# A new order of all operations of a gated recurrence with a highway layer behind it

## The chip, the cores and the metric

The kernel runs on one core of one Trainium2 chip. The metric is the device time of one execution in microseconds. The kernel before took 205.67 us, the median of 3 runs (205.38 to 205.77).

## The reference

The input is x (4 sequences of 6336 steps, 256 channels), gate logits of the same shape, and a lower bound per channel. The first half is a gated recurrence along each sequence; its result goes, token by token, through a highway layer with two 256x256 weights.

```
sig = sigmoid(f_logit)
f = lower_bound + (1 - lower_bound) * sig ; i = 1 - f
h = f[:, t] * h + i[:, t] * x[:, t] ; y[:, t] = h          # for t in 6336 steps, h = 0 at the start of each sequence
H = relu(y @ w_h) ; T = sigmoid(y @ w_t + b_t)
out = T * H + (1 - T) * y
```

## The kernel before

The 25344 tokens are cut into 29 units of 2, 4 or 8 blocks of 128 tokens (`parts`, L42): two units of 2 blocks, three of 4, twenty-two of 8, then one of 4 and one of 2. The 256 channels are two halves of 128; h or m (0 or 1) is the half. Every unit passes through the same operations, each of which is one short function, `do_` and a letter:

- l and x load the unit's logits and inputs (both queued on SP). One load fetches units 0 and 1 together.
- u (ACT): u = sigmoid(-logit), which is 1 - sig. b (POOL, or DVE): the product bv = u * x. Both have tokens on the partitions.
- i and p (PE): transposes of u and of bv, so that channels lie on the partitions (uT and bT, in PSUM).
- f (ACT, or DVE): f = 1 + ncc * uT, with ncc = lower_bound - 1 per channel.
- s (DVE): the recurrence, as a scan y = f * y + bT along the tokens. The factor 1 - lower_bound is left out of bv and comes in later, in the weights and in diag. A scan carries on from the scan of the same half in the unit before.
- z and g (PE): the two matmuls of the highway layer. Both need the y of both halves.
- t (ACT): t = sigmoid(z + b_t). d (DVE): d = max(ncc * y, g), which is relu(y @ w_h) - y, since the identity has been taken from w_h (IW, on POOL). e (POOL, or DVE): d = d * t, in pieces of 256 to 2048 columns.
- o (PE): transposes y and d back and adds them, through diag (cc on the diagonal) and an identity. c (ACT, or DVE): copies the result out of PSUM. w: the store, queued on SP (the very last one on ACT).

Besides there are single ones: the weight loads wh and wt, their scaling WH (DVE) and WTa (ACT), lbT and tbT (pc and pb: the bounds and biases turned), cc, cb, IW, dgp, and k, idle matmuls on PE.

What sets the order is a text of 847 tokens, `order`, written out by hand or by a search and read from left to right (L49 and L401). In `s4.1:2`, s is the operation, 4 the unit, 1 the half (or the piece), and 2 the buffer that its output takes. A `v` at the end puts b, f, e or c on DVE instead of POOL or ACT. `k*3:a0` is three idle matmuls into buffer a0. Each engine runs its operations strictly in the order of their tokens and waits only for data and for buffers. In PSUM, i and p share the two buffers a0 and a1, so a uT can be written when the scan has read the bT that lay there; z, g and o share b0, b1 and b2 (and in the last units a0 and a1). Six buffers hold l and six hold x. Loads and stores leave SP in the order of their tokens, and a store that waits for its c holds up the loads behind it.

One more rule is in `shared` (L173): after a product on DVE (b or e) the next product on POOL in the text waits until it is done.

Of the kernel before, what the change touches and what calls it, by code (L numbers as in the profile page):

```python
# [53 lines left out]
t2.0:2 b3.1:7 d2.0:2 e1.0 e0.0 x6:5 e2.0v p3.1:1 i4.0:0 s3.1:7 e0.1 l7:0 g2.1:0 u5:1 f4.0:0 z2.1:1 o1.0:2 i4.1:1 x7:0 t2.1 d2.1 i5.1:0
l8:1 b4.1:1 b4.0v:0 e2.1v g3.0:0 f4.1:2 x8:1 g3.1:1 i5.0:1 f5.1:1 p4.1:0 d3.0:1 d3.1 z3.0:0 s4.1:2 o0.0:1 l9:2 f5.0:3 c1.0:0 p4.0:1
z3.1:2 s4.0:3 t3.0:1 c0.0:1 t3.1 b5.1:2 u6:2 p5.1:0 b5.0:3 l11:3 x9:2 e3.0 z4.1:0 z4.0:1 t4.1:0 e3.1 t4.0 p5.0:1 s5.1:0 o2.0:2 s5.0:1
i6.1:0 g4.1:0 c2.0:2 f6.1:2 o3.0:1 d4.1:0 w0.0 w2.0 g4.0:2 b6.1:4 i6.0:1 c3.0:3 p6.1:0 w3.0 b6.0:5 u7:3 d4.0 f6.0:0 z5.0:0 g5.0:2
s6.1:4 d5.0:2 t5.0:2 z5.1:1 p6.0:0 i7.1:1 e4.0 b7.1:6 s6.0:5 f7.1:1 t5.1 g5.1:2 d5.1 p7.1:1 g6.1:0 i7.0:0 e4.1 o4.0:1 b7.0:7 u8:0
f7.0:3 c4.0:4 z6.1:2 e5.0 p7.0:0 s7.1:6 e5.1 b8.0:1 i8.1:1 d6.1:1 s7.0:7 t6.1:1 z6.0:1 e6.2 g6.0:0 d6.0 w1.0 f8.1:2 l10:4 i8.0:1
f8.0v:0 z7.0:2 u9:1 i9.1:0 t6.0 f9.1:1 g7.1:0 p8.0:1 x10:3 i9.0:0 l12:5 z7.1:1 e6.1v u11:2 f9.0:3 e5.2v e6.0v d7.1:0 t7.1:0 b8.1:0  # L60
s8.0:2 o6.1:0 c6.1:1 p8.1:0 o6.0:1 t7.0 i11.1:1 g7.0:0 b9.0:2 c6.0:2 u10:3 s8.1:3 d7.0 p9.0:0 f11.1:0 b9.1:3 e7.2 o5.0:2 c5.0:3 o5.1:1
g8.0:0 e7.1 p9.1:1 c5.1:0 s9.0:4 i10.0:0 x11:4 l14:0 l13:1 d8.0:1 z8.1:2 z8.0:1 f10.0:2 g8.1:0 t8.1:2 s9.1:5 b10.0:4 d8.1 p10.0:0
s10.0:0 w6.1 t8.0 b10.1:5 b11.1:6 e7.0 g9.1:2 i10.1:1 w4.0 z9.0:1 e8.1 u12:0 d9.1:2 w5.1 g9.0:0 f10.1:3 i11.0:0 t9.0:1 p10.1:1 x12:5
f11.0:1 l15:2 o7.1:1 w5.0 x13:0 b11.0:7 e8.2 u13:1 e8.0 d9.0 s10.1:1 z9.1:2 p11.1:0 o7.0:0 i13.1:1 t9.1 g10.0:2 c7.0:1 z10.0:0 s11.1:6
f13.1:2 i12.1:1 c7.1:4 b12.0:1 p11.0:0 t10.0:0 z10.1:1 d10.0:0 f12.1:3 g10.1:2 s11.0:7 d10.1 b12.1:0 t10.1 i12.0:1 e9.0v o8.1:0 g11.0:1
# [373 lines left out]
```

## Time and profile before

The profile is of one execution on the chip. Its own time was 205.4 us, 0.3 us under the median of the three runs; the span from its first to its last instruction is 203.6 us.

| | busy, us | instructions |
|---|---|---|
| PE (matmul) | 187.2 | 1784 |
| DVE | 191.4 | 154 |
| ACT | 193.6 | 202 |
| POOL | 172.7 | 104 |
| HBM | 52.43 MB read, 25.95 MB written | 385 GB/s over the span |

A row of the timeline gives start and length in us, engine, line, what is written from what, and in brackets the engine's idle time before it with what ended it. Lengths overlap: an instruction's record is some 0.05 to 0.4 us longer than the step to the next one's start when nothing waits, so steps from start to start are the better price. Rows of windows give busy time of PE, PEld, DVE, ACT and POOL with the count of instructions, the granted clock, the share of the DMA engines and GB/s.

### The profile page before, as it was taken

How to read it: one execution, taken by the hardware profiler on the slowest of the kernel's cores; microseconds unless marked ns; L12 is line 12 of the kernel's file. 1: busy time of each engine (PE TensorE's matmuls, PEld its weight loads, DVE VectorE, ACT ScalarE, POOL GpSimd, SP SyncE). 2: the span in 40 equal slices, each digit the busy share in tenths (PEclk: the TensorE clock that was granted, in tenths of full speed). 3: DMA queues.
4: the chain of work that ended last, by engine and by line, in shares of the span. 5: the costliest groups of instructions: out<-in, count | busy, mean ns of one | idle time of the engine just before them, and what ended most of it. 6: DMA issues, size and time to landing. Idle time of an engine off the chain costs nothing.

```text
span 203.6 us, 4577 instructions
## 1 busy us (share of the span) xinstructions
PE 187.2 (92%) x1784; PEld 130.9 (64%) x1812; DVE 191.4 (94%) x154; ACT 193.6 (95%) x202; POOL 172.7 (85%) x104
## 2 busy tenths in 40 slices
...
DMA  6999999999999999999999999999999996858876
GB/s 195 396 417 427 412 415 430 409 410 430 412 414 428 394 424 414 434 417 423 427 406 428 424 412 424 427 419 421 421 422 408 313 422 253 279 192 335 354 306 263
DMA packets 16381, 78.68 MB, mean 386 GB/s; under 512 B 1764, under 2 KB 2536, under 8 KB 10728
## 3 DMA queue, kind: packets, MB, share of 16 engines
...
q8 instruction: 14, 0.23, 0.4%
...
q14 instruction: 7, 0.06, 0.1%
HBM read 52.43 MB, written 25.95 MB: 385 GB/s over the span
## 4 chain that ended last, share of the span: by engine, by line
PE 44%; DVE 28%; ACT 10%; issue 8%; DMA 7%; SPq 0%; DVEq 0%; ACTq 0%
DVE y L323 17%; DVE d L352 7%; PE op L380 7%; PE op L381 6%; PE z L335 6%; PE g L335 6%; PE bT L304 6%; PE uT L284 5%; DMA out_dram<-o 5%; PE g L111 5%; PE z L111 4%; ACT f L295 3%; ACT u L268 3%; ACT t L348 2%; DMA x<-in_x_dram 2%
## 5 line engine op out<-in xcount | busy, mean ns | idle before, releaser
L276 POOL TENSOR_TENSOR bv<-u,x 128x1024 bf16<-128x1024 f16 (+2 forms) x54 | 103.9, 1945 | 12.6 <-DVE d L358 12.1
L323 DVE TENSOR_TENSOR_SCAN y<-f,y,bT 128x1024 bf16<-128x1024 f16 (+5 forms) x56 | 107.0, 1928 | 0.5 <-PE bT L304 0.4
L358 POOL TENSOR_TENSOR d<-d,t 128x512 bf16<-128x512 bf16 (+3 forms) x35 | 66.3, 1905 | 4.7 <-DVE d L358 3.5
L352 DVE SCALAR_TENSOR_TENSOR d<-y,ncc,g 128x1024 bf16<-128x1024 bf16 (+2 forms) x58 | 63.4, 1108 | 0.6 <-PE g L111 0.4
L348 ACT ACTIVATE t<-z,bt 128x1024 bf16<-128x1024 f32 (+2 forms) x58 | 62.3, 1105 | 0.5 <-PE z L111 0.2
L295 ACT ACTIVATE f<-uT,ncc 128x1024 f16<-128x1024 f16 (+2 forms) x55 | 60.6, 1112 | 0.9 <-PE uT L284 0.9
L393 ACT COPY o<-op 128x1024 f32<-128x1024 f32 (+2 forms) x56 | 53.5, 1010 | 1.4 <-PE op L381 1.4
L268 ACT ACTIVATE u<-l 128x2048 f16<-128x2048 f32 (+2 forms) x29 | 51.5, 1779 | 1.7 <-DMA l<-in_f_logit_dram 1.7
L380 PE MATMUL op<-diag,y 128*128 128x128 f16 x396 | 49.5, 219 | 1.2 <-DVE d L352 0.8
L381 PE MATMUL op<-ident_b,d 128*128 128x128 bf16 x396 | 49.6, 219 | 0.1
L381 PEld LDWEIGHTS <-d 128*128 128x128 bf16 x396 | 44.1, 113 | 4.4 <-issue 2.5
L380 PEld LDWEIGHTS <-y 128*128 128x128 bf16 x396 | 44.2, 113 | 2.0
L335 PE MATMUL z<-y,w_sb 128*128 128x512 bf16 (+1 forms) x112 | 38.9, 368 | 2.7 <-ACT t L348 0.7
L335 PE MATMUL g<-y,w_sb 128*128 128x512 bf16 (+1 forms) x112 | 38.7, 367 | 1.1 <-ACT o L393 0.7
L304 PE MATMUL bT<-ident_f,bv 128*128 128x128 f32 x198 | 31.9, 277 | 3.8 <-DVE y L323 1.4
L284 PEld LDWEIGHTS <-u 128*128 128x128 f16 x396 | 26.6, 98 | 11.2 <-issue 4.3
L284 PE MATMUL uT<-ident_h,u 128*128 128x128 f16 x396 | 31.4, 219 | 1.9 <-DVE y L323 1.7
L335 PEld LDWEIGHTS <-w_sb 128*128 128x128 f16 x232 | 22.0, 98 | 16.3 <-DVE y L323 0.9
L111 PE MATMUL g<-y,w_sb 128*128 128x512 bf16 x84 | 31.8, 379 | 0.1
L304 PEld LDWEIGHTS bT<-ident_f,bv 128*128 128x128 f32 x198 | 22.4, 141 | 12.8 <-issue 4.1
L111 PEld LDWEIGHTS <-w_sb 128*128 128x128 f16 x176 | 17.2, 98 | 17.4 <-issue 3.6
L111 PE MATMUL z<-y,w_sb 128*128 128x512 bf16 x72 | 27.3, 379 | 0.1
...
## 6 DMA issues: line engine op xcount, KB each, us to landing
out_dram<-o SPq DMA_DIRECT2D x48, 512.0 KB, 10.0
...
out_dram<-o SPq DMA_DIRECT2D x2, 256.0 KB, 16.0
...
```

The lines of the kernel that those rows point to most:

```text
L111: return pe.add_instruction(mybir.InstMatmult(name=nc.get_next_instruction_name(), start_tensor_calc=start, stop_tensor_calc=stop, tile_si ...
L276: shared(pin(e.tensor_mul(bv[:, :nb // 2].rearrange("p k d j -> p k j d"), st[n]["u"][:, :nb, own].rearrange("p (k j) d -> p k j d", j=2), ...
L284: pin(nc.tensor.transpose(uT[:, j * P:(j + 1) * P], st[n]["u"][:, j, h * P:(h + 1) * P], ident_h))
L295: pin(nc.scalar.activation(to, of, AF.Identity, scale=ncc[:, h:h + 1], bias=1.0))
L304: pin(nc.tensor.transpose(words[:, k:k + g * (P - 1) + 1:g], pair, ident_f))
L323: pin(nc.vector.tensor_tensor_scan(y[:, c:e], st[n]["f", h][:, c:e], st[n]["bT", h][:, c:e], 0.0 if fresh else carry[h], op0=ALU.mult, op1 ...
L335: pin(nc.tensor.matmul(p[:, a:e], w, half(n, "y", ki)[:, a:e], start=ki == 0, stop=ki == NH - 1))
L348: pin(nc.scalar.activation(half(n, "t", m), st[n]["z", m][:, :tokens(n)], AF.Sigmoid, bias=bt[:, m:m + 1]))
L352: pin(nc.vector.scalar_tensor_tensor(half(n, "d", m), half(n, "y", m), ncc[:, m:m + 1], st[n]["g", m][:, :tokens(n)], op0=ALU.mult, op1=AL ...
L358: shared(pin(e.tensor_mul(st[n]["d"][:, a:c], st[n]["d"][:, a:c], st[n]["t"][:, a:c])), not eng)
L380: pin(nc.tensor.matmul(o, half(n, "y", h)[:, cols], diag[:, h], start=True, stop=False))
L381: pin(nc.tensor.matmul(o, half(n, "d", h)[:, cols], ident_b, start=False, stop=True))
```

## The change

Only the text `order` is replaced, and it is one line longer, so all lines of the kernel behind it move by one. Both texts have the same 847 operations but for the idle matmuls. Units, buffers, rules and functions stay as they were. In the text

- all operations may stand at another place, and many take another buffer;
- on DVE instead of POOL are now b1.1, e5.1, e24.1 and e25.2, and on POOL instead of DVE e6.1, e26.2 and e27.0; f3.1 is on DVE instead of f2.1; c27.0 is on DVE instead of ACT;
- there are 15 idle matmuls instead of 12. Before: 3, 2, 2, 2, 2 among the first units and 1 at unit 14. After: 3 and 4 ahead of the first transpose, 2 and 2 among the first units, 3 and 1 at units 6 to 8;
- wt is loaded ahead of wh;
- the first stores stand behind l10 instead of ahead of it, and later loads and stores are interleaved in another order.

The first two lines of the text show what the diff is like:

```
-l0:0 k*3:a0 pc:0 cc k*2:a1 pb:1 k*2:a0 u0:0 x0:0 u1:1 b0.0v:0 wh i0.1:1 f0.1:0 i1.0:0 k*2:2 b0.1v:1 cb i0.0:1 f1.0:1 b1.0v:2 f0.0:2 wt
-IW p0.1:0 b1.1:3 WTa k*2:0 p0.0:1 s0.1:0 i1.1:0 l2:1 s0.0:1 p1.0:1 f1.1:3 WH x2:1 s1.0:2 u2:2 p1.1:0 g0.0:2 z0.1:1 i2.1:1 dgp l3:2
...
+l0:0 k*3:a0 u0:0 k*4:a1 x0:0 pc:0 cc i0.1:0 u1:1 i1.0:1 pb:1 wt f0.1:0 b0.1v:0 f1.0:1 k*2:2 i0.0:0 f0.0:2 WTa b1.0v:1 wh b0.0v:2
+b1.1v:3 cb l2:1 p0.1:1 IW k*2:0 p0.0:0 x2:1 s0.1:0 l3:2 i1.1:1 s0.0:1 f1.1:3 WH p1.1:0 x3:2 z0.0:2 g0.0:1 s1.1:2 u2:2 t0.0:0 p1.0:1
```

and the lines around unit 18, where the second bT (p18.1) follows the first z of unit 17 instead of both z and the uT i19.1:

```
-o14.0:0 s17.1:5 c14.1:4 p18.0:0 b19.0:6 i18.1:1 z16.1:1 d16.0 c14.0:0 f18.1:0 g17.1:2 t16.1 i20.0:1 z17.0:0 f20.0:3 w12.1 t17.0:2
-b19.1:7 s18.0:0 w13.0 b20.0:0 d17.1:1 z17.1:1 l22:3 e16.0v t17.1 i19.1:0 p18.1:1 w14.1 u21:0 x21:2 b20.1:1 w14.0 g17.0:2 o16.1:0
...
+w12.1 w11.0 x20:1 d15.1 u20:1 f19.0:0 o14.0:1 s17.1:5 c14.0:4 g16.0:0 p18.0:0 c14.1:2 i18.1:1 f18.1:2 d16.0 z16.1:1 g17.1:0 b20.1:0
+i20.0:1 t16.1 z17.0:2 s18.0:0 l21:2 d17.1:2 e16.0v w13.0 w12.0 w13.1 p18.1:0 s18.1:1 f20.0:3 i19.1:1 z17.1:1 t17.0:2 x21:2 f19.1:1
```

Three places of the built programs show how the engines' own orders move. First DVE in the head, from its first product on; bv is b, y is s, w_sb is WH, f is f, d is d. Before:

```order
L276 TENSOR_TENSOR bv_118<-u_112,x_114 128x2x128
L276 TENSOR_TENSOR bv_132<-u_112,x_114 128x2x128
L202 COPY bt_90<-tbT_107 128x2
L276 TENSOR_TENSOR bv_140<-u_116,x_114 128x2x128
L323 SCALAR_TENSOR_TENSOR y_158<-f_124,bT_147 128x256
L323 SCALAR_TENSOR_TENSOR y_165<-f_142,bT_156 128x256
L225 TENSOR_SCALAR w_sb_92<-w_raw_91,cc_88 128x256 x2
L323 SCALAR_TENSOR_TENSOR y_175<-f_138,y_165,bT_167 128x256
L323 SCALAR_TENSOR_TENSOR y_196<-f_169,y_158,bT_179 128x256
L293 TENSOR_SCALAR f_207<-uT_187,ncc_89 128x512
L352 SCALAR_TENSOR_TENSOR d_230<-y_165,ncc_89,g_181 128x256
L352 SCALAR_TENSOR_TENSOR d_232<-y_196,ncc_89,g_222 128x256
```

and with the change:

```order
L277 TENSOR_TENSOR bv_126<-u_100,x_107 128x2x128
L277 TENSOR_TENSOR bv_140<-u_116,x_107 128x2x128
L277 TENSOR_TENSOR bv_143<-u_100,x_107 128x2x128
L277 TENSOR_TENSOR bv_145<-u_116,x_107 128x2x128
L203 COPY bt_90<-tbT_121 128x2
L324 SCALAR_TENSOR_TENSOR y_161<-f_124,bT_150 128x256
L324 SCALAR_TENSOR_TENSOR y_168<-f_136,bT_157 128x256
L226 TENSOR_SCALAR w_sb_92<-w_raw_91,cc_88 128x256 x2
L324 SCALAR_TENSOR_TENSOR y_184<-f_170,y_161,bT_174 128x256
L324 SCALAR_TENSOR_TENSOR y_195<-f_128,y_168,bT_190 128x256
L353 SCALAR_TENSOR_TENSOR d_209<-y_168,ncc_89,g_181 128x256
L353 SCALAR_TENSOR_TENSOR d_209<-y_161,ncc_89,g_192 128x256
```

DVE makes all four products of units 0 and 1, and both d of unit 0 stand where an f of unit 2 and one d stood.

Second, DVE in the last units, from the d of unit 27 on (d_2998 and d_3028 are unit 27; d_3093 and d_3089 unit 28; a product d<-d,t is e). Before:

```order
L352 SCALAR_TENSOR_TENSOR d_2998<-y_2880,ncc_89,g_2979 128x512
L323 SCALAR_TENSOR_TENSOR y_3000<-f_2719,y_2880,bT_2996 128x256
L323 SCALAR_TENSOR_TENSOR y_3036<-f_2709,y_2939,bT_3023 128x256
L352 SCALAR_TENSOR_TENSOR d_2998<-y_2939,ncc_89,g_3038 128x512
L358 TENSOR_TENSOR d_2998<-d_2998,t_2977 128x512 x2
L352 SCALAR_TENSOR_TENSOR d_3093<-y_3036,ncc_89,g_3071 128x256
L352 SCALAR_TENSOR_TENSOR d_3093<-y_3000,ncc_89,g_3074 128x256
L358 TENSOR_TENSOR d_3093<-d_3093,t_3060 128x256 x2
```

and with the change:

```order
L353 SCALAR_TENSOR_TENSOR d_3028<-y_2923,ncc_89,g_3010 128x512
L353 SCALAR_TENSOR_TENSOR d_3028<-y_2990,ncc_89,g_3016 128x512
L324 SCALAR_TENSOR_TENSOR y_3068<-f_2687,y_2990,bT_3040 128x256
L359 TENSOR_TENSOR d_3028<-d_3028,t_3013 128x512
L353 SCALAR_TENSOR_TENSOR d_3089<-y_3068,ncc_89,g_3075 128x256
L392 COPY o_3107<-op_3078 128x512
L353 SCALAR_TENSOR_TENSOR d_3089<-y_2996,ncc_89,g_3101 128x256
L359 TENSOR_TENSOR d_3089<-d_3089,t_3087 128x256 x2
```

The last scan stands behind both d of unit 27, one e of unit 27 has gone, and the copy c27.0 stands between the two d of unit 28.

Third, the last operations of ACT (o<-op is c, t is t). Before:

```order
L348 ACTIVATE t_3060<-z_3057,bt_90 128x256
L393 COPY o_3054<-op_3062 128x512
L348 ACTIVATE t_3060<-z_3077,bt_90 128x256
L393 COPY o_3114<-op_3084 128x512
L393 COPY o_3114<-op_3095 128x512
L393 COPY o_3122<-op_3108 128x256
L393 COPY o_3124<-op_3116 128x256
```

and with the change:

```order
L349 ACTIVATE t_3087<-z_3071,bt_90 128x256
L394 COPY o_3107<-op_3092 128x512
L349 ACTIVATE t_3087<-z_3104,bt_90 128x256
L394 COPY o_3121<-op_3116 128x256
L394 COPY o_3129<-op_3123 128x256
```

c27.0 is no longer there, and c27.1 stands ahead of the last t, so that behind the last t only the two copies of unit 28 are left.

More of the change, by code (lines that the diff above doesn't have):

```diff
@@ L54 @@
[L54 to L65, printed above, removed]
@@ L90 @@
-p27.0:0 d25.1 s27.0:2 k*0:1 z26.0:1 c24.1:4 g26.1:0 e24.1 t26.0:2 b27.1:7 e25.0v d26.1:1 e25.2 o24.0:2 f27.1:2 p27.1:0 w23.0 w21.0
-b28.0:1 b28.1:2 c24.0:3 z26.1:1 s27.1:3 o25.2:a1 g26.0:0 e25.1v t26.1 o25.3:a0 d26.0 z27.1:2 w24.1 c25.2:2 z27.0:1 c25.3 t27.1:0
-g27.0:a1 e26.2v w23.1 t27.0 w24.0 e26.0v o25.1:0 p28.0:0 d27.0:0 s28.0:6 c25.1:1 e26.1 o25.0:2 o26.3:1 p28.1:1 c25.0 o26.2:0 w25.1
-s28.1:7 g27.1:2 c26.3:4 c26.2 d27.1 o26.0:1 c26.0:0 e27.0v z28.1:a0 t28.1:1 o26.1:a1 g28.1:0 g28.0:2 z28.0:1 w25.0 e27.1v c26.1 t28.0
@@ L94 @@
-o27.0:a0 d28.1:2 o27.1:0 d28.0 e28.1v e28.0v w26.1 o28.1:2 w26.0 c27.0:3 o28.0:a1 c27.1 c28.1:2 c28.0:1 w27.0 w28.1 w28.0
+l0:0 k*3:a0 u0:0 k*4:a1 x0:0 pc:0 cc i0.1:0 u1:1 i1.0:1 pb:1 wt f0.1:0 b0.1v:0 f1.0:1 k*2:2 i0.0:0 f0.0:2 WTa b1.0v:1 wh b0.0v:2
+b1.1v:3 cb l2:1 p0.1:1 IW k*2:0 p0.0:0 x2:1 s0.1:0 l3:2 i1.1:1 s0.0:1 f1.1:3 WH p1.1:0 x3:2 z0.0:2 g0.0:1 s1.1:2 u2:2 t0.0:0 p1.0:1
+g0.1:0 s1.0:3 l4:3 b2.1:4 i2.1:0 g1.0:2 d0.0:0 f2.1:0 d0.1 i2.0:1 d1.0:1 p2.1:0 l5:4 z1.1:1 s2.1:4 b2.0:5 f2.0:2 e0.0 z1.0:0 p2.0:1
```

65 lines of the change are left out of this document (41 added, 24 removed).

## The prediction

> **What bounds the kernel now.** I read the page first, then busy time by stage, then the first 30 us and the last 40 us of the timeline, then who waited for whom. Each fence shows one of these.
>
> ```profile
> PE 187.2 (92%) x1784; PEld 130.9 (64%) x1812; DVE 191.4 (94%) x154; ACT 193.6 (95%) x202; POOL 172.7 (85%) x104
> DMA  6999999999999999999999999999999996858876
> ```
>
> Three engines and the DMA queues are all above 90%, so the share says little. The stages tell more (columns: busy time of PE, PEld, DVE, ACT, POOL, clock, DMA share, GB/s):
>
> ```profile
> 24.00:159.00 135.00, 127.92 (x1233) 90.46 (x1254) 134.59 (x90) 135.00 (x124) 124.27 (x58) 1.00 1.02 419
> 159.00:199.00 40.00, 39.63 (x421) 29.74 (x425) 38.94 (x36) 38.14 (x48) 31.69 (x21) 1.00 0.81 306
> ```
>
> From 24 to 159 us ACT is busy 135.00 of 135.00: it paces this stage, with DVE 0.41 us behind. From 159 to 199 us the pacemaker is PE, 39.63 of 40.00, while ACT and DVE have 1.9 and 1.1 us free. So the span is a head, an ACT stage, a PE stage and a last store. What sets the head:
>
> ```profile
> 6.01 0.78 DVE L276 TENSOR_TENSOR bv<-u,x 128x256 bf16<-128x256 f16 x2 [1.65 <-DMA x<-in_x_dram]
> 10.08 2.29 POOL L276 TENSOR_TENSOR bv<-u,x 128x512 bf16<-128x512 f16 x2 [0.20 <-DMA x<-in_x_dram]
> 11.80 2.46 DVE L323 TENSOR_TENSOR_SCAN y<-f,y,bT 128x512 bf16<-128x512 f16 x2
> 8.69 0.33 SPq L256 DMA_DIRECT2D l<-in_f_logit_dram  x1
> DMA to landing us min/median/max: 15.2/15.2/15.2
> 23.99 1.94 ACT L268 ACTIVATE u<-l 128x2048 f16<-128x2048 f32 x1
> ```
>
> DVE starts at 6.01 because x0 lands. The first scan of unit 2 (11.80) follows the landing of x2, through POOL's product from 10.08. The load l6, issued at 8.69, takes 15.2 us and lands at 23.9; u6 starts at 23.99. From there ACT never rests.
>
> **The change part by part.**
>
> *Head.* The loads up to l11 keep their order and sizes; only the two 256 KB weight loads change places. All of them leave through one queue on DMA engines that are full from 5 us on, so x0, x2 and l6 should land as before: price 0. Between 6.01 and 11.80 DVE gets one more 256-wide product (b1.1, from POOL) and a third 256-wide d, and loses a 512-wide f (f2.1, now on ACT; f3.1 comes to DVE in its place, later):
>
> ```profile
> 7.28 1.26 DVE L323 TENSOR_TENSOR_SCAN y<-f,bT 128x256 bf16<-128x256 f16 x2
> 10.38 0.72 DVE L293 TENSOR_SCALAR f<-uT,ncc 128x512 f16<-128x512 f16 x1
> 11.02 0.86 DVE L352 SCALAR_TENSOR_TENSOR d<-y,ncc,g 128x256 bf16<-128x256 bf16 x2
> 21.66 6.93 DVE L323 TENSOR_TENSOR_SCAN y<-f,y,bT 128x512 bf16<-128x512 f16 x4 [0.18 <-PE bT L304]
> 29.88 2.35 DVE L323 TENSOR_TENSOR_SCAN y<-f,y,bT 128x1024 bf16<-128x1024 f16 x1
> 27.84 1.18 ACT L295 ACTIVATE f<-uT,ncc 128x1024 f16<-128x1024 f16 x1
> ```
>
> By start-to-start steps: +0.37 for b1.1, -0.64 for f2.1, +0.39 for the third d, so +0.1 before 11.80, where DVE had 0.1 to 0.2 of waits to give. Behind 11.80 it has 0.64 - 0.39 = 0.25 us more work and, in the old order, 0.4 us of waits up to 21.66. It meets the same wall at 29.88 in any case: s6.1 needs f6.1 (made from 27.84 on), which stands fourth behind u6 on ACT in both orders, and the bT whose buffer f6.1 frees. Head: 0, bounds -0.1 and +0.3.
>
> *Seven idle matmuls ahead of the lbT transpose instead of three* (and 15 in all instead of 12):
>
> ```profile
> 2.41 0.63 PE L122 MATMUL idle<-const-bfloat16-1.0 128*128 128x512 bf16 x1
> 2.84 1.06 PE L111 MATMUL idle<-const-bfloat16-1.0 128*128 128x512 bf16 x2
> 4.02 0.61 PE L122 MATMUL idle<-const-bfloat16-1.0 128*128 128x512 bf16 x1
> 5.17 0.39 PE L122 MATMUL idle<-const-bfloat16-1.0 128*128 128x512 bf16 x1
> 5.62 0.49 PE L284 MATMUL uT<-ident_h,u 128*128 128x128 f16 x4
> 5.93 1.31 ACT L295 ACTIVATE f<-uT,ncc 128x256 f16<-128x256 f16 x3 [0.23 <-PE uT L284]
> ```
>
> They stand 0.43 us apart until the clock is granted shortly before 5.17, and 0.22 after. Seven from 2.41 end at about 5.2; lbT and ncc follow by 5.6, before the first f (5.93) reads ncc. Cover: the wait for x0 until 6.01. If the clock came one matmul later the price is 0.2 us, and the landing of x2 hides that. Four more dummies at 38 to 41 us cost 0.9 us of a PE that has 7.1 us free in that stage. Price 0.
>
> *ACT stage.* Between u6 and the f that frees PE's bank for i24.1, ACT runs the same 123 operations in both orders, only permuted. With no idle time in it, a permutation gains nothing; it can lose where a uT, z or op comes late. DVE's one real wait in this stage goes away, since p18.1 now stands ahead of z17.1 and i19.1 on PE (1.3 us of work), but that gives DVE slack, not time:
>
> ```profile
> 124.85 2.35 DVE L323 TENSOR_TENSOR_SCAN y<-f,y,bT 128x1024 bf16<-128x1024 f16 x1 [0.25 <-PE bT L304]
> ```
>
> Price 0; bounds 0 and +0.3 (one DVE wait like this one turned into ACT's).
>
> *PE stage.* It begins when ACT has made f23.0:
>
> ```profile
> 157.60 1.35 ACT L295 ACTIVATE f<-uT,ncc 128x1024 f16<-128x1024 f16 x1
> 159.04 0.61 PE L284 MATMUL uT<-ident_h,u 128*128 128x128 f16 x8
> ```
>
> From i24.1 on both orders hold the same PE groups: 9 i, 11 p, 13 z, 14 g, 22 o. The old order leaves PE idle 0.37 us of 40.00 here, so a new one can gain 0.4 at most. I take 0; bounds -0.4 and +0.6, the latter from DVE, next.
>
> *DVE's last 19 us.* c27.0, a 512-wide copy out of PSUM, moves from ACT to DVE; e26.2 and e27.0 go to POOL, e24.1 and e25.2 come (four times 512, even).
>
> ```profile
> L391 DVE COPY o<-op 128x1024 f32<-128x1024 f32 x1 | 1.2, 1217 | 0.0
> 179.38 2.34 DVE L323 TENSOR_TENSOR_SCAN y<-f,y,bT 128x1024 bf16<-128x1024 f16 x1
> 183.13 2.34 DVE L323 TENSOR_TENSOR_SCAN y<-f,y,bT 128x1024 bf16<-128x1024 f16 x1
> 185.38 1.26 DVE L352 SCALAR_TENSOR_TENSOR d<-y,ncc,g 128x1024 bf16<-128x1024 bf16 x1
> 186.58 1.28 DVE L323 TENSOR_TENSOR_SCAN y<-f,y,bT 128x512 bf16<-128x512 f16 x1
> 191.53 1.28 DVE L352 SCALAR_TENSOR_TENSOR d<-y,ncc,g 128x1024 bf16<-128x1024 bf16 x1 [0.24 <-PE g L111]
> 197.96 0.49 DVE L358 TENSOR_TENSOR d<-d,t 128x256 bf16<-128x256 bf16 x2
> ```
>
> Half of the 1024-wide copy is about 0.62 us. From 179.38 to 198.45 DVE takes 19.07 us; its instructions by their unhindered steps (2.25 a 1024-wide scan, 183.13 to 185.38; 1.2 a 1024-wide d, to 186.58; and so on) come to 18.16, so 0.91 is waiting, mostly for PE. With the copy it has 18.78 of work: it fits in 19.07 if it waits no more than 0.29. I take that as hidden, price 0. If the old waits stay, +0.62.
>
> *The very end.*
>
> ```profile
> 198.16 0.30 DVE d L358
> 198.51 0.23 PE op L381
> 198.89 0.21 ACT o L393
> 199.11 0.54 ACT o L393 x2
> 198.03 1.63 ACT L393 COPY o<-op 128x512 f32<-128x512 f32 x4
> ```
>
> The last e ends at 198.45, PE's last op follows, but ACT is still in c27.1 until 199.0. Without c27.0, c27.1 is over before the last op is there (first op ready 198.8): -0.2 us. The store behind it stays.
>
> Sum against the profiled run: span 203.6 - 0.2 = 203.4, with the 1.8 us around it (205.4 - 203.6) 205.2. That run lies 0.27 under the median of 205.67, so the median forecast is 205.5.
>
> *A rule weighed.* In the trace the 512-wide product that DVE began at 190.75 took 0.55 us, against 0.41 at 44.80, and POOL was in a product until 191.02:
>
> ```profile
> 190.75 0.55 DVE L358 TENSOR_TENSOR d<-d,t 128x512 bf16<-128x512 bf16 x1
> 189.71 1.31 POOL L276 TENSOR_TENSOR bv<-u,x 128x256 bf16<-128x256 f16 x2
> 44.80 0.41 DVE L358 TENSOR_TENSOR d<-d,t 128x512 bf16<-128x512 bf16 x1
> ```
>
> The Trainium skill, page "SBUF — State Buffer", section "SBUF: two separate sides", says that a DVE instruction with two SBUF inputs and a GpSimd instruction hold one port pair exclusively, and that the later one waits for the other's end. The trace agrees with it here: the product ended 0.27 us after POOL's did. With the delay that this row shows, 0.14 us, the sum would be 205.6; with the longest that the rule allows beside a 512-wide POOL product, 1.17 us, it would be 206.7.
>
> **The rivals.**
>
> *Faster, 205.0 (chance 0.32).* PE's bubbles in the last stage go: -0.2 - 0.4 gives 205.1, and 0.1 more if DVE's 0.3 us of slack in the last 19 us reaches the end. For it: e24.1, e25.2 and e25.0 now come before s27.0, so the op groups of units 24 and 25 wait less, and POOL has both halves of e26 earlier (before, POOL idled 2.9 us ahead of its last product). Against it: PE can't start this stage before ACT lets it.
>
> *Slower, 206.2 (chance 0.22).* DVE instead of PE sets the end. In the last 3 us the copy sits between d28.1 and d28.0, so every wait of DVE is passed on to the last op. d28.1 now comes one e (0.34) behind s28.1, where d27.1 and two e's (1.4 us) stood between; z28.1 and g28.1 at 0.2 us each, and their way through PSUM at about as much again, don't fit into 0.34, so d28.1 waits some 0.3. It decides from 0.29 us of waiting on. If the old waits of 0.91 stay, the end moves by +0.62 - 0.2 = +0.4; with the new one on top by +0.7; the middle gives 206.2. Against it: DVE's old waits were for g, which PE now reaches with other work ahead of it.
>
> *A port collision, 205.9 (chance 0.06).* e27.1 on DVE comes 0.66 + 0.64 = 1.3 us behind d27.0 on DVE's line, and POOL's e27.0, let go by d27.0, takes 1.17. Start it 0.5 late and DVE stands 0.4: 0.4 behind 205.5.
>
> *The reordering moves nothing that counts* is the forecast itself (chance 0.40, its own range 205.2 to 205.9).
>
> **How the numbers follow.** 0.2% is 0.41 us, about what a measurement here tells from no change: under 205.26 is faster, over 206.08 slower. Faster is 0.30 of the faster rival's 0.32 and 0.05 of the forecast's 0.40: 0.35. Slower is 0.20 of the slower rival's 0.22, half of the collision's 0.06 and 0.02 of the forecast: 0.25. The rest, 0.40, is the same. The range goes down by the PE stage's 0.4, the end's 0.2 and the head's 0.1 to 205.0, and by 0.3 more for DVE's slack in the last 19 us to 204.7; it goes up by +0.62 + 0.3 - 0.2 to 206.4.
>
> **What would show it.** u6 again at 23.9 to 24.0 and s6.1 at 29.9: head right. ACT with no idle time between 24 and 159, i24.1 at 158.5 to 159.5: stage right. PE over 39.5 of 40 in the last stage: right; below 39 with DVE waits on g or op: the slower rival. c28.1 right behind the last op: the 0.2. Wrong at the root would be an i24.1 over 0.5 us earlier, which would mean that ACT's full row hid slack, or landings that moved.

## The result, and the profile after

The change made the kernel slower: 206.79 us, the median of 17 executions, against 205.42 for 17 of the kernel before; ratio 1.0059, 95% interval 1.0039 to 1.0080. The prediction of 205.5 (204.7 to 206.4) was wrong. The spread changed as much as the median: the kernel before lies between 205.20 and 205.77, the changed one between 205.23 and 208.48. Its best execution is as good as the best before; most are not. Medians here and below are over all executions, while the ratios leave out those over 1.5% above the fastest of their kernel: 208.37 and 208.48 us here, and further down 208.85, 208.93, and three that stand in no range of the table either, 879.7 and 1074.14 (of the kernel before) and 490.2 (of the kernel with four loads of the middle early, the one that was profiled).

The profiled execution took 206.88 us with a span of 205.1, so 1.5 more span than before (203.6). Its page has these shares:

```profile
PE 189.2 (92%) x1788; PEld 131.4 (64%) x1815; DVE 192.6 (94%) x156; ACT 192.9 (94%) x201; POOL 171.6 (84%) x103
DMA  6999999999999999999999999999998997985867
```

The work is much the same: DVE has 1.2 us more of it, PE 2.0, ACT and POOL 0.7 and 1.1 less, and no engine is busy for more than 94% of the span. So most of the time went into waits, and the windows say in which stage (columns as in the prediction):

```profile
24.00:159.00 135.00, 127.93 (x1236) 90.57 (x1255) 134.60 (x90) 134.88 (x123) 124.72 (x58) 1.00 1.01 414
159.00:199.00 40.00, 39.02 (x402) 28.41 (x405) 38.09 (x33) 36.35 (x44) 32.21 (x21) 1.00 0.82 302
```

From 24 to 159 us nothing moved: ACT 134.88 (135.00 before), DVE 134.60 (134.59). In the last stage PE got 0.6, DVE 0.85 and ACT 1.8 us less done. The timeline of ACT and DVE there; first the row of the kernel before that counts most, the sigmoid of unit 27 (u27):

```profile
177.88 1.07 ACT L268 ACTIVATE u<-l 128x1024 f16<-128x1024 f32 x1
```

and with the change u27 and the two scans of unit 26:

```profile
180.00 1.06 ACT L269 ACTIVATE u<-l 128x1024 f16<-128x1024 f32 x1 [1.51 <-DMA l<-in_f_logit_dram]
179.85 2.34 DVE L324 TENSOR_TENSOR_SCAN y<-f,y,bT 128x1024 bf16<-128x1024 f16 x1
184.72 2.35 DVE L324 TENSOR_TENSOR_SCAN y<-f,y,bT 128x1024 bf16<-128x1024 f16 x1 [1.35 <-PE bT L305]
```

u27 starts at 180.00 after ACT has stood 1.51 us for the landing of unit 27's logits; before, it started at 177.88 and waited for nothing. DVE feels it one scan later: s26.0 starts 0.47 us later than before (179.38), s26.1 1.59 later (183.13). Its landing, in the rows of SyncE's queue and in the answer on that one load; first the kernel before:

```profile
172.27 0.42 SPq L256 DMA_DIRECT2D l<-in_f_logit_dram  x1
DMA to landing us min/median/max: 4.9/4.9/4.9
```

and with the change:

```profile
170.92 2.27 SPq L399 DMA_DIRECT2D out_dram<-o  x3
173.24 0.73 SPq L257 DMA_DIRECT2D l<-in_f_logit_dram  x1
DMA to landing us min/median/max: 6.7/6.7/6.7
```

l27 leaves 0.97 us later, behind three stores (w21.1, w21.0, w20.1) and not one, and takes 6.7 us and not 4.9: it lands at 179.97 instead of 177.2. The order wanted it at 178.49.

The account of the 1.5 us by start times: +0.47 is there at s26.0, brought from the head; +1.12 comes at s26.1, from l27; +1.13 comes on DVE from s26.1 to its last e (16.45 us, 15.32 before); and some 1.1 comes back at the very end, which the last store of each kernel shows, before

```profile
199.69 0.38 ACTq L398 DMA_DIRECT2D out_dram<-o  x1
```

and with the change:

```profile
198.85 0.48 DVE L353 SCALAR_TENSOR_TENSOR d<-y,ncc,g 128x256 bf16<-128x256 bf16 x1 [0.41 <-PE g L336]
199.40 0.69 DVE L392 COPY o<-op 128x512 f32<-128x512 f32 x1
200.46 0.71 DVE L359 TENSOR_TENSOR d<-d,t 128x256 bf16<-128x256 bf16 x2
202.33 0.38 ACTq L399 DMA_DIRECT2D out_dram<-o  x1
```

The last store is issued 2.64 us later, but the span ends only 1.5 later: 2.8 us behind that store instead of 3.9. Before, the last stores followed each other within 0.6 us (199.13 to 199.69) and queued; now they come apart (200.5, 202.05, 202.33).

### The profile page after: what moved, and what is told of

Read it like the earlier page. It is cut to its first block, busy times and chain, and to the rows that moved or that the text cites. A ratio compares the mean times of both kernels' runs of the same rounds, so it can differ in the third digit from the quotient of the medians.

```text
span 205.1 us, 4595 instructions
## 1 busy us (share of the span) xinstructions
PE 189.2 (92%) x1788; PEld 131.4 (64%) x1815; DVE 192.6 (94%) x156; ACT 192.9 (94%) x201; POOL 171.6 (84%) x103
## 5 line engine op out<-in xcount | busy, mean ns | idle before, releaser
L349 ACT ACTIVATE t<-z,bt 128x1024 bf16<-128x1024 f32 (+2 forms) x58 | 59.0, 1043 | 1.1 <-PE z L112 0.5
L296 ACT ACTIVATE f<-uT,ncc 128x1024 f16<-128x1024 f16 (+2 forms) x55 | 57.4, 1053 | 2.0 <-PE uT L285 1.8
L394 ACT COPY o<-op 128x1024 f32<-128x1024 f32 (+2 forms) x55 | 51.0, 962 | 1.9 <-ACT t L349 1.5
L269 ACT ACTIVATE u<-l 128x2048 f16<-128x2048 f32 (+2 forms) x29 | 49.6, 1712 | 3.0 <-DMA l<-in_f_logit_dram 3.0
L336 PE MATMUL g<-y,w_sb 128*128 128x512 bf16 (+1 forms) x115 | 40.0, 368 | 1.3 <-DVE y L324 0.3
L336 PE MATMUL z<-y,w_sb 128*128 128x512 bf16 (+1 forms) x114 | 39.5, 368 | 1.8 <-ACT t L349 0.7
L112 PE MATMUL z<-y,w_sb 128*128 128x512 bf16 x80 | 30.3, 379 | 0.0
L112 PE MATMUL g<-y,w_sb 128*128 128x512 bf16 x72 | 27.3, 379 | 0.0
```

Of the source, the lines that this page charges most:

```text
L112: return pe.add_instruction(mybir.InstMatmult(name=nc.get_next_instruction_name(), start_tensor_calc=start, stop_tensor_calc=stop, tile_si ...
L296: pin(nc.scalar.activation(to, of, AF.Identity, scale=ncc[:, h:h + 1], bias=1.0))
L336: pin(nc.tensor.matmul(p[:, a:e], w, half(n, "y", ki)[:, a:e], start=ki == 0, stop=ki == NH - 1))
L349: pin(nc.scalar.activation(half(n, "t", m), st[n]["z", m][:, :tokens(n)], AF.Sigmoid, bias=bt[:, m:m + 1]))
```

## The experiments

Runs of one group shared a chip and the runs of the kernel before. Ratios are to those, with their 95% interval. Only groups 1 and 3 have the changed kernel itself beside the edited ones, so elsewhere the loss is compared across groups, by the ratios. The expectations call the engines ScalarE (ACT), VectorE (DVE), GpSimd (POOL), TensorE (PE) and SyncE (SP). Most kernels ran 12 times; 6 times "before, l27 late", 10 times "l27 ahead of three stores", 11 times the last of group 3, and 23 to 35 times the kernel before.

| group, kernel | median, us | lowest to highest | ratio |
|---|---|---|---|
| 1 kernel before | 205.91 | 205.43 to 207.23 | 1 |
| 1 changed kernel again | 207.29 | 205.93 to 208.78 | 1.0064 (1.0035 to 1.0093) |
| 1 l27 ahead of three stores | 207.15 | 205.95 to 208.55 | 1.0060 (1.0034 to 1.0086) |
| 1 c27.0 on ACT | 206.48 | 205.67 to 208.01 | 1.0032 (1.0008 to 1.0056) |
| 1 b1.1 on POOL | 206.93 | 205.87 to 207.33 | 1.0036 (1.0018 to 1.0055) |
| 2 kernel before | 205.90 | 205.53 to 206.72 | 1 |
| 2 before, l27 late | 207.12 | 207.00 to 207.60 | 1.0058 (1.0043 to 1.0074) |
| 2 four loads of the middle early | 206.42 | 205.82 to 208.02 | 1.0028 (1.0005 to 1.0050) |
| 2 x26 and l27 early | 205.96 | 205.42 to 208.93 | 1.0024 (0.9993 to 1.0054) |
| 2 all six early | 206.88 | 205.70 to 208.39 | 1.0040 (1.0012 to 1.0067) |
| 3 kernel before | 206.00 | 205.36 to 206.75 | 1 |
| 3 changed kernel again | 206.95 | 205.53 to 208.85 | 1.0043 (1.0017 to 1.0069) |
| 3 changed, five stores less | 206.59 | 205.46 to 207.30 | 1.0033 (1.0014 to 1.0052) |
| 3 before, five stores less | 206.07 | 205.81 to 206.81 | 1.0016 (1.0005 to 1.0027) |
| 3 changed, five stores less, x26 and l27 early | 205.53 | 205.38 to 205.78 | 0.9984 (0.9974 to 0.9995) |
| 4 kernel before | 206.08 | 205.61 to 206.98 | 1 |
| 4 before, two loads of the middle late | 206.15 | 205.75 to 206.57 | 1.0003 (0.9989 to 1.0016) |
| 4 the last of group 3 again | 205.76 | 205.38 to 207.07 | 0.9993 (0.9977 to 1.0008) |
| 4 the same, lbT early | 205.74 | 205.32 to 206.35 | 0.9989 (0.9975 to 1.0003) |
| 4 the same, c27.0 on ACT | 205.70 | 205.38 to 206.10 | 0.9984 (0.9972 to 0.9995) |
| 5 kernel before | 206.11 | 205.57 to 207.29 | 1 |
| 5 all six early again | 206.80 | 205.43 to 207.50 | 1.0026 (1.0006 to 1.0046) |
| 5 the same, l17 apart | 206.50 | 205.67 to 207.24 | 1.0018 (0.9999 to 1.0037) |

The first theory was that l27's landing costs what it is late. The rivals: VectorE's last microseconds, with the copy c27.0, and the head.

**The yardstick of group 1**: the changed kernel, not edited.

> The changed kernel once more, as the yardstick of this group. Load theory (unit 27's input of f lands after its sigmoid on ScalarE is due): 206.2 to 207.3 with a spread of over 1 us, and the profiled run's own time goes with the length of ScalarE's wait for that landing (1.5 us in the first profile). End theory (the copy c27.0 and the waits of the last 3 us on VectorE set it): the same median, but a landing that differs by half a microsecond or more between the two profiles leaves the time where it was.

The profiled execution (206.61 us) waited 0.91 us for l27, not 1.51, and its span is 0.3 shorter. (The third profile of the changed kernel, of group 3, goes the other way by the same rule: a wait of 1.73 us and a span 0.4 longer.) The spread is nearly 3 us: 205.93 to 208.78.

**l27 ahead of all three stores.**

```diff
-s25.0:4 w21.1 w21.0 d24.1:0 f28.1:0 w20.1 c22.0:2 z24.0:2 p25.1:0 l27:3 b26.1:5
+s25.0:4 l27:3 w21.1 w21.0 d24.1:0 f28.1:0 w20.1 c22.0:2 z24.0:2 p25.1:0 b26.1:5
```

> The changed kernel with one token moved: the load of unit 27's f goes on SyncE's queue ahead of the three stores w21.1, w21.0 and w20.1 instead of behind them, 3.75 us of transfers at 420 GB/s. Load theory: it lands before 177.5, ScalarE's wait of 1.5 us is gone, s26.1 starts at 183.6 instead of 184.7, and 1.1 us comes back less what waits behind it: 205.6 to 206.1, with a spread under 0.8 us. End theory: the wait is gone too, but VectorE's last 3 us keep their waits and the time stays within 0.3 of the changed kernel. Head theory (0.5 us lost before 31 us is all that counts): s6.1 still at 30.5, and time within 0.3 of the changed kernel as well.

A miss. The wait for l27 is gone, but a new one stands a few operations ahead of it in ACT's line:

```profile
176.27 1.01 ACT L394 COPY o<-op 128x1024 f32<-128x1024 f32 x1 [1.47 <-DMA out_dram<-o]
179.80 1.07 ACT L269 ACTIVATE u<-l 128x1024 f16<-128x1024 f32 x1
```

c22.0 needs the buffer whose content w21.1 stores, and w21.1 now stood behind l27 and landed at 176.19. u27 started at 179.80, as late as ever. A load that passes a store pushes back the copy that waits for that store: the same lateness, paid at another place.

**c27.0 back on ACT.**

```diff
-d28.1:1 w26.1 o27.1:a0 g28.0:2 z28.0:0 c27.0v:1 w26.0 c27.1
+d28.1:1 w26.1 o27.1:a0 g28.0:2 z28.0:0 c27.0:1 w26.0 c27.1
```

> The changed kernel with the copy c27.0 back on ScalarE, nothing else. End theory: VectorE's 0.69 us copy between its last combinations is gone, the last store starts 0.5 to 0.9 us earlier, 206.0 to 206.3. Load theory: ScalarE's wait for unit 27's landing stays 1 us or more, the end gains at most 0.3, 206.4 to 207.0 with the spread of over 1 us.

206.48 looks like a gain of 0.8 us, but this kernel has the same wide spread, and its profiled execution (207.61) lost 1.5 us by 160 us to late landings that have nothing to do with the copy. A version of the changed kernel that hardly spreads, further down, decides it: the quiet version.

**b1.1 back on POOL.**

```diff
-b1.1v:3 cb l2:1 p0.1:1 IW
+b1.1:3 cb l2:1 p0.1:1 IW
```

> The changed kernel with the product b1.1 back on GpSimd. Head theory: VectorE has 0.34 us less to do between 6 and 12 us, s2.1 starts at 11.8 or before (12.00 with the change) and s6.1 at 30.1 to 30.3 (30.56), the time falls by 0.2 to 0.4. Load theory: the head's gain is real but the landing of unit 27's f decides; time within 0.3 of the changed kernel, spread of over 1 us.

s2.1 started at 12.22, now waiting 0.28 for an f, and s6.1 at 30.67: the head gained nothing by it. The product b1.1 is not what the head lost. The median is 0.36 us lower, which is well within the spread.

In the profiles of this group loads land late in the middle too, by amounts that differ between executions. Between landing and first use l14, x17, x15, x26 and l27 had 14.4, 1.9, 1.0, 1.4 and 0.7 us before, and l22 at least 1.9 (the store behind it landed then). In the first profile of the changed order they have 0.08, 0.13, 0.37, 0.13, 0.02 and, l22, 0.08, and where the figure is smallest the engine had been waiting (0.38 us for x17, 1.51 for l27). So the theory became: executions differ by how far the queue of transfers has fallen behind, and the changed order has no slack for it. A caution stands against it from the start: the kernel before has tight loads as well (l16 0.22, l26 0.36, x16 0.55 us), and spreads far less.

**The kernel before, with l27 behind three stores.**

```diff
-t24.1 w21.1 l27:3 f28.0:0
+t24.1 w21.1 w21.0 w19.1 l27:3 f28.0:0
```

> The kernel before, with the stores w21.0 and w19.1 put ahead of the load of unit 27's f on SyncE's queue (they stood behind it). Landing theory (a load with no slack at the end costs what it is late, less what the rest gives back): that load lands at 178.5 to 179.7 instead of 177.2, ScalarE waits 0.6 to 1.8 us for it, 0.3 to 1.0 us slower than the kernel before. Rival (the end is set by VectorE's last 3 us or by the head): ScalarE waits, but the time stays within 0.2 of the kernel before.

1.2 us slower, a little more than expected, and steady (207.0 to 207.6, in 6 executions). The one edit reproduces the changed kernel's loss at the end: ACT waits as long as there,

```profile
179.79 1.06 ACT L268 ACTIVATE u<-l 128x1024 f16<-128x1024 f32 x1 [1.37 <-DMA l<-in_f_logit_dram]
182.93 1.28 DVE L352 SCALAR_TENSOR_TENSOR d<-y,ncc,g 128x1024 bf16<-128x1024 bf16 x1 [0.78 <-PE g L111]
```

and the wait reaches DVE through PE. So a late l27 costs the old order 1.2 us; what it costs the changed one group 3 shows. By these six executions it does not make the spread.

**Four loads of the middle earlier, the two of the end earlier, and all six.** The end's edit leaves w21.1 ahead of l27, for the reason just found.

```diff
-w6.1 p10.1:0 i11.0:1 l14:1
+l14:1 w6.1 p10.1:0 i11.0:1
...
-d11.1 w5.0 t11.0 u15:2 i14.1:0 x15:2
+d11.1 x15:2 w5.0 t11.0 u15:2 i14.1:0
...
-w11.1 p15.0:0 o11.0:1 b16.0:0 x17:4
+x17:4 w11.1 p15.0:0 o11.0:1 b16.0:0
...
-w13.0 w12.0 w13.1 ... x21:2 ... l22:3
+w13.0 w12.0 l22:3 w13.1 ... x21:2
```

```diff
-l28:2 u26:3 ... w20.0 ... x26:1
+l28:2 x26:1 u26:3 ... w20.0
...
-w21.1 w21.0 d24.1:0 f28.1:0 w20.1 c22.0:2 z24.0:2 p25.1:0 l27:3
+w21.1 l27:3 w21.0 d24.1:0 f28.1:0 w20.1 c22.0:2 z24.0:2 p25.1:0
```

> The changed kernel with four loads of the middle each put ahead of one or two stores on SyncE's queue: l14, x15, x17 and l22, whose landings stood 0.08 to 0.37 us ahead of their use. Landing theory: transfers run at 420 GB/s without a gap from 10 to 155 us, so each hiccup of theirs becomes a stall where the slack is 0.1; with 1.2 us or more of slack the four waits are gone, VectorE's offset between 78 and 160 us stays at that of s6.1, the spread falls from 2.9 to below 2 us and the median by 0.2 to 0.6. Rival (the spread comes from the tail or from TensorE's clock): spread and median stay within 0.2 of the changed kernel.

> The changed kernel with the loads x26 and l27 alone put ahead of the stores w20.0, and w21.0 and w20.1, on SyncE's queue (not ahead of w21.1, whose landing ScalarE's copy of c22.0 awaits). Landing theory: x26 lands near 170.3 and l27 near 176 instead of 173.0 and 180.0, no copy waits for a store, the waits of 0.4 and 1.5 us are gone, s26.1 starts at 183.6 to 183.9, and the time falls by 0.4 to 1.1 us; a spread of 1 to 2 us from the middle stays. Rival (the end of VectorE decides): the waits are gone and the time stays within 0.2.

> The changed kernel with the six loads of the two runs before moved together, nothing else. Landing theory: no wait for a landing from 24 us on, the spread falls to 1 us or less, and the time comes to within 0.5 of the kernel before (the head's 0.5 us on VectorE stays). Rival theories (head, VectorE's end, TensorE's clock): 1 us or more above the kernel before, with the spread of the changed kernel.

By the ratios (1.0028, 1.0024 and 1.0040 against 1.0064 in group 1) each took off a third to three fifths of the loss, but the intervals overlap that of group 1, and none ended the spread: 2.2, 3.5 and 2.7 us. For the two of the end alone what was expected of the spread (1 to 2 us) was missed as well. The execution profiled with all six loads early was a good one (205.75 us): no engine waits for a load from 24 us on, and against the changed kernel the end comes back as expected:

```profile
178.42 1.07 ACT L269 ACTIVATE u<-l 128x1024 f16<-128x1024 f32 x1
183.76 2.35 DVE L324 TENSOR_TENSOR_SCAN y<-f,y,bT 128x1024 bf16<-128x1024 f16 x1 [0.37 <-PE bT L305]
```

The one with the end's two loads early was a bad one (208.43 us), and shows what the middle can cost. The rows in which ACT and POOL wait for a transfer:

```profile
71.06 1.91 ACT L269 ACTIVATE u<-l 128x2048 f16<-128x2048 f32 x1 [0.75 <-DMA l<-in_f_logit_dram]
106.96 4.28 POOL L277 TENSOR_TENSOR bv<-u,x 128x1024 bf16<-128x1024 f16 x2 [1.57 <-DMA x<-in_x_dram]
168.52 1.91 ACT L269 ACTIVATE u<-l 128x2048 f16<-128x2048 f32 x1 [0.84 <-DMA l<-in_f_logit_dram]
174.24 1.01 ACT L394 COPY o<-op 128x1024 f32<-128x1024 f32 x1 [0.37 <-DMA out_dram<-o]
```

These are l14, x17 and l26, and the copy of c22.0; s26.0 started at 182.33, 2.5 us later than in the first profile of the changed kernel. The DMA rows of its window 84 to 100 us, in slices of 0.4 us, show where x17's lateness came from:

```profile
DMA  8999999999999999896949799899999999999999
GB/s 369 399 451 410 420 410 451 389 430 430 420 451 410 430 451 410 287 389 184 266 143 348 256 389 338 317 410 379 389 471 440 379 430 399 410 399 451 410 399 440
```

From 90.4 to 94.4 us the slices show 143 to 389 GB/s. Over these 4.0 us together the DMA engines are busy 0.98 of the time and move 292 GB/s, where they move 421 from 84.0 to 90.4: a stretch of slow transfers, during l17 and x16. In the same window of the kernel before no slice is below 328.

But six moved loads did not narrow the spread (205.70 to 208.39), as the theory had said they would. Either the slack was still too small, at these loads or at others (l26, for which ACT waits above, is not one of the six), or the spread was not made by transfers. Moving loads can't tell, since every store that is passed is a buffer that comes free later. Taking transfers away can.

**The changed kernel a third time, and both kernels without the stores of units 0 to 4.**

> The changed kernel a third time, as the yardstick of this group: 206.2 to 207.3 by all theories, with a spread of over 2 us.

```diff
-z6.1:0 w1.0 g6.1:1 ... s7.0:7 w0.0 k*3:1 ... t6.0 w4.0 k*1:a1 ... i9.1:0 w3.0 z7.1:2 ... f10.1:3 w2.0 w6.0
+z6.1:0 g6.1:1 ... s7.0:7 k*3:1 ... t6.0 k*1:a1 ... i9.1:0 z7.1:2 ... f10.1:3 w6.0
```

> The changed kernel without the stores of units 0 to 4 (w0.0, w1.0, w2.0, w3.0 and w4.0: 2.1 MB, whose rows of the output are not written), nothing else. That takes 5.0 us of transfers at 420 GB/s out of the queue before 65 us, and every later load may be 5 us later in its queue before it is late. Lateness theory (executions differ by how far slow stretches of transfers put the queue behind, 2 to 4 us by 150 us, and the changed order has 0.08 to 0.4 us of slack at six loads): the spread falls below 1.2 us, no wait for l14, x17 and l22 is left, and the median comes down by 0.6 or more against the changed kernel of this group. Rival (the spread comes from TensorE's clock, the products on GpSimd or the tail alone): spread of 2 us and more, median within 0.3.

> The kernel before without the same five stores, the control. Lateness theory: its loads have slack enough as they are (0.2 us at the least, 0.5 to 2 at most), so the 5.0 us of transfers are worth nothing: within 0.3 of the kernel before, spread as narrow. Rival (both kernels are held up by the transfers of the middle alike): it gains as much as the changed kernel does, 0.6 or more.

The changed kernel gained 0.36 us on its median against the yardstick and 1.5 on its worst execution (208.85 to 207.30). That is half of what the theory had asked for, the spread of 1.8 us is above its 1.2, and the intervals of the two ratios overlap: by itself this run decides nothing. In its profiled execution (205.79 us) the loads of the middle that have a recorded landing have 1.2 us of slack and more, and one wait for a load is left:

```profile
179.08 1.06 ACT L269 ACTIVATE u<-l 128x1024 f16<-128x1024 f32 x1 [0.40 <-DMA l<-in_f_logit_dram]
```

The control gained nothing (1.0016, if anything a little lost): in the old order these transfers held up nobody.

**The same with the end's two loads early.** Units 0 to 4 are not stored here either. The edit to the end is that of group 2.

> The changed kernel without those five stores and with the loads x26 and l27 ahead of w20.0, and of w21.0 and w20.1. Lateness theory: what the run without stores leaves of the loss stands at unit 27's f, so this one is another 0.3 to 1.0 us faster than that run, and at or under the kernel before (ratio 0.996 to 1.001). Rival (head of 0.5 us and VectorE's end of 1.1 us remain): it stays 0.5 or more above the kernel before.

205.53 us, 205.38 to 205.78: as the theory had said. Loss and spread are both gone, and the ratio is under 1. (Repeated in group 4: 205.76, ratio 0.9993, eleven of twelve executions within 0.8 us.) This is the quiet version. In its profile there is no wait for a load behind 24 us:

```profile
171.13 0.42 SPq L257 DMA_DIRECT2D l<-in_f_logit_dram  x1
DMA to landing us min/median/max: 4.6/4.6/4.6
178.19 1.07 ACT L269 ACTIVATE u<-l 128x1024 f16<-128x1024 f32 x1
183.53 2.35 DVE L324 TENSOR_TENSOR_SCAN y<-f,y,bT 128x1024 bf16<-128x1024 f16 x1 [0.35 <-PE bT L305]
200.72 0.39 ACTq L399 DMA_DIRECT2D out_dram<-o  x1
```

By group 3 the end's two loads are worth 1.1 us (206.59 to 205.53), and the 5 us of transfers 0.4 on the median, which is not clear of noise. The spread takes both: with the end's loads early but all stores it was 3.5 us (group 2, with waits for l14, x17 and l26 in the profile), with the stores gone but the end's loads late 1.8, with both 0.4 (1.7 in the repetition, through one execution). The slow stretches have not gone, in fact: the same window of 84 to 100 us in this execution reads

```profile
GB/s 246 256 287 317 348 348 410 451 328 430 328 369 246 225 205 328 328 307 389 430 451 420 420 440 369 481 379 379 451 369 451 430 389 461 358 461 389 420 430 430
```

with 205 to 348 GB/s in 14 of the first 18 slices. From 24 to 159 us this execution even moved less per us than the first one of the changed kernel (400 GB/s, 414 there). The slow stretches are simply not felt: every load behind 24 us whose landing is recorded lands 1.1 us or more ahead of its use.

**The kernel before, with two loads of the middle behind a store each.**

```diff
-x15:2 l16:4 c10.0:1 u17:0 ... w9.1 s13.1:5 w9.0 i14.0:1 x16:3 w8.0
+x15:2 c10.0:1 u17:0 ... w9.1 l16:4 s13.1:5 w9.0 i14.0:1 w8.0 x16:3
```

> The kernel before with two loads of the middle put behind a store each on SyncE's queue: l16 behind w9.1, and x16 behind w8.0. By a queue at 420 GB/s l16 lands 0.8 us and x16 0.5 us after they are wanted, where they had 0.2 and 0.6 us of slack. If any order of transfers has the slow stretches, and the kernel before only had slack for them: ScalarE waits 0.8 to 1.5 us for l16, the median is 0.7 to 1.5 us above the kernel before, and the spread widens to 1.5 us and more. If the slow stretches belong to the changed order of transfers: the same median, with a spread of 0.8 us or less. If a late load of the middle is worth nothing: within 0.2 of the kernel before.

Weaker than meant. The waits came out small,

```profile
91.59 1.92 ACT L268 ACTIVATE u<-l 128x2048 f16<-128x2048 f32 x1 [0.20 <-DMA l<-in_f_logit_dram]
96.59 4.28 POOL L276 TENSOR_TENSOR bv<-u,x 128x1024 bf16<-128x1024 f16 x2 [0.32 <-DMA x<-in_x_dram]
```

and cost 0.36 us by s26.0 in this execution (offset against the first profile of before: 0.33 at s13.1, 0.69 from s21.0 on), which the median does not show. The spread stayed narrow (0.8 us), though both loads had no slack at all. By the expectation that would speak for slow stretches that belong to the changed order. But the control of group 3, the old order without five stores, has one in its profile too: 285 GB/s from 62.8 to 66.0 us, where the kernel before moves 429. So slow stretches don't belong to the changed order alone, and why two loads without slack do not spread the old order stays open.

**The small prices, on the quiet version.** First its repetition as a yardstick, then lbT (the turned lower bounds, from which DVE makes ncc) ahead of the four idle matmuls behind u0, then c27.0 on ACT; the five stores are left out in all three.

```diff
-u0:0 k*4:a1 x0:0 pc:0 cc i0.1:0
+u0:0 x0:0 pc:0 cc k*4:a1 i0.1:0
```

> The changed kernel without the five stores and with x26 and l27 early, once more, as the yardstick of this group: 205.3 to 205.7 with a spread below 0.8 us.

> The yardstick with lbT ahead of the four idle matmuls behind u0 instead of behind them (three before it, as the kernel before had). If the idle matmuls ahead of lbT cost the head its 0.3 to 0.5 us: ncc starts at 4.1 instead of 5.8, s6.1 comes 0.2 us or more sooner after the first load, and the time falls by 0.2 to 0.5. If they cost nothing, as predicted: ncc at 4.1 and the time within 0.1 of the yardstick, since the products b0.1 and b1.0 wait for x0 until 6.0 anyway.

> The yardstick with the copy c27.0 back on ScalarE. If the copy on VectorE costs the end its 0.69 us (the rival Slower): the time falls by 0.3 to 0.7. If it is hidden, as predicted: within 0.15 of the yardstick. If it relieves ScalarE (the end waits on ScalarE's copies): 0.2 to 0.6 slower.

The yardstick has one execution at 207.07, the other eleven lie within 0.8 us. lbT early changes nothing: ncc starts 1.45 us sooner and DVE then waits for x0. The yardstick's first rows on DVE,

```profile
5.58 0.16 DVE L196 TENSOR_SCALAR ncc<-lbT 128x2 f32<-128x2 f32 x1 [5.58 <-PE lbT L190]
6.31 1.45 DVE L277 TENSOR_TENSOR bv<-u,x 128x256 bf16<-128x256 f16 x4 [0.50 <-DMA x<-in_x_dram]
```

and with lbT early:

```profile
4.13 0.16 DVE L196 TENSOR_SCALAR ncc<-lbT 128x2 f32<-128x2 f32 x1 [4.13 <-PE lbT L190]
6.44 1.45 DVE L277 TENSOR_TENSOR bv<-u,x 128x256 bf16<-128x256 f16 x4 [2.08 <-DMA x<-in_x_dram]
```

c27.0 on ACT changes nothing either (205.70 against 205.76). DVE takes as long from s26.1 to its last e (16.07 us, 16.03 with the copy). So the 0.8 us of group 1 are put down to the spread.

**What makes the slow stretch at 91 us.** l17 ahead of w8.1, in the kernel with all six loads early, so that l17 and x16 are not loaded one behind the other.

```diff
-w9.1 t12.0:1 ... c10.1:2 w8.1 g13.0:0 d12.0 d13.0:0 l17:4 z13.0:1
+w9.1 l17:4 t12.0:1 ... c10.1:2 w8.1 g13.0:0 d12.0 d13.0:0 z13.0:1
```

> The changed kernel with all six loads moved (l14, x15, x17, l22, x26, l27), once more, as the yardstick of this group: 206.0 to 207.0 with a spread of 2 us or more.

> The yardstick with l17 ahead of the store w8.1 instead of behind it, so that l17 and x16 (2 MB of loads back to back, whose packets were slow from 90 to 95 us in the executions that lost most) no longer follow each other. If the slow stretch at 91 us comes from these two loads one behind the other: no slow stretch there, spread below 1.2 us, median 0.4 or more under the yardstick and within 0.2 of the kernel before or under it. If it comes with the place in time or with l17's rows, or the spread is made elsewhere: spread and median as the yardstick, within 0.3.

Within 0.3 us of its yardstick, with a spread of 1.6 us against 2.1: by the expectation not these two loads. Neither of the two profiled executions has the slow stretch (413 and 415 GB/s from 90.4 to 94.4 us), so the traces can't decide it, and its cause stays open. The second one shows something else: ACT waits 0.52 us for l26, which none of the edits moved. In the first profile with all six early l26 had landed 1.02 us ahead of its use, in the yardstick's 0.02. So a seventh load had no slack that lasts, which is one reason why moving six did not end the spread. No version with all its stores was shown to beat the kernel before.

## Why the prediction was wrong, step by step

**Loads, the step that failed.** The prediction priced landings only up to l11 ("should land as before: price 0") and put those behind it at nothing without a word, although the page it began with shows the DMA row at 9 from 10 to 155 us and the windows 419 GB/s. Its last lines name "landings that moved" as a sign of being wrong, but only for an i24.1 that comes earlier. On transfers that run without a gap, a load that is put behind more stores lands later by their time (in the kernel before, two more stores of 512 KB put l27's use at 179.79 behind a landing that had been at 177.2: 2.6 us), and SyncE's order was part of the change. The missing term at the end was l27: +1.1 us by the start times, 1.1 by group 3 (together with x26), 1.2 by one edit in the kernel before. In the middle it was a slack of 0.1 us at l14, x17 and l22: up to 1.5 us in a bad execution, and some 0.4 on the median, the latter not clear of noise. Why transfers run slow for some us in some executions is not known.

**Head, 0 with bounds -0.1 and +0.3.** u6 came at 24.16 (23.9 to 24.0 was said), and s6.1 at 30.56 instead of 29.9. In the changed order u6 does not hang on l6: with lbT early l6 landed 1.4 us ahead of its use, and u6 started at 24.38; in its yardstick l6 came just in time, and u6 started at 24.35. The wall at 29.88 was not one. The prediction took it for the moment at which f6.1 lets the scan go; the rows that it quotes (21.66 and 6.93, then 29.88) and the one of the kernel before between them,

```profile
28.50 1.38 DVE L352 SCALAR_TENSOR_TENSOR d<-y,ncc,g 128x512 bf16<-128x512 bf16 x2
```

show DVE without idle time up to 29.88. So what DVE lost by s4.1 stayed lost; with the change:

```profile
19.30 0.99 DVE L277 TENSOR_TENSOR bv<-u,x 128x512 bf16<-128x512 f16 x1
22.17 2.44 DVE L324 TENSOR_TENSOR_SCAN y<-f,y,bT 128x512 bf16<-128x512 f16 x2
18.53 1.17 POOL L277 TENSOR_TENSOR bv<-u,x 128x512 bf16<-128x512 f16 x1
```

s4.1 is 0.51 late (22.17, 21.66 before). 0.20 of it is there at s2.1 (12.00, 11.80 before), where the prediction had +0.1 hidden by waits. 0.26 is one product, b4.0, which took 0.99 us where it had taken 0.73. Over all profiles s6.1 stands at 30.40 to 30.86 in the changed order (15 of them, mean 30.63) and at 29.88 to 30.30 in the old one (4, mean 30.15), so the head costs about 0.5. It does not reach the end by itself: in the quiet version s26.0 was 0.28 late and the span 203.6, as before.

The rule weighed in the prediction is at work in that product. In both kernels b4.0 ended 0.6 us behind the end of POOL's product (20.29 behind 19.70; before, 19.86 behind 19.25). In all 19 profiles it ends 0.59 to 0.61 us behind POOL's end, though it starts 0.75 to 1.04 us behind POOL's start: it waited for POOL and then ran, and the price is how early it starts. The Trainium skill, "SBUF — State Buffer", section "SBUF: two separate sides", says just that of two inputs from SBUF; the trace agrees, at another place than the one that the prediction feared. e27.1, the rival there, took 0.40: no delay to be seen.

**Seven idle matmuls, 0.** Right on the whole, and for the reason given: with lbT early DVE only waits longer for x0. But the seven end at 5.6 and not at 5.2, lbT and ncc come at 5.5 and 5.8 ("by 5.6"), and in this execution x0 had landed at 5.74, so that the first product may have stood 0.1 us for ncc.

**ACT stage, 0.** Right in the profiled execution: ACT 134.88 of 135.00, and the offset of DVE's scans is +0.51 at s4.1 and +0.47 at s26.0. The bound of +0.3 was not: in the bad execution shown above s24.1, the first scan behind 168 us, was 1.5 us later still.

**PE stage, -0.4 to +0.6.** PE came to 39.02, under the 39.5 that was named as right. Not PE's or DVE's own order, but l27: with no load late PE has 39.75 (the quiet version) and 40.00 (its repetition).

**DVE's last 19 us, hidden; the very end, -0.2.** The copy is free, as predicted, but not because DVE has 0.29 us to spare: with c27.0 back on ACT, DVE's last stretch is no shorter. In the quiet version DVE takes 0.7 us longer from s26.1 to its last e, the last store is issued at 200.72 instead of 199.69, and the span still ends at 203.6. The end belongs to the stores: "the store behind it stays" was wrong by 1 us, in favour of the change. From the end of the last e to the last store it is 1.16 us instead of 1.24, so of the 0.2 not half came.

**Rivals.** Slower (206.2) had the direction and less than half of the size (+0.5 us, measured +1.4), with the wrong mechanism: c27.0 on ACT gave nothing back. Faster (205.0) is what the order itself may do once no load is late: in group 3 the two kernels without the five stores, one with its loads in time, differ by 0.5 us (205.53 and 206.07). Against the kernel before, which stores all, the quiet version stands at 0.9984 and, repeated, at 0.9993, where 1 is within the interval; so that gain is not shown.
